# Attention, capacity MoE and a cosine MLP on one core: expert products of 448 columns, routing counts shared by two engines, an earlier gate

## The chip, the core and the metric

The kernel runs on one core of a Trainium2 chip. The metric is the device time of one execution in microseconds (us): the time before is the median of three runs, 1180.96 us (1175.52 to 1181.75). A profiled execution stands beside them.

## What is computed

Three stages follow one another, all in float32 (the reference, cut to what matters):

```python
# attention: q, k, v are (4, 12, 448, 64)
q_n, k_n = rmsnorm(q, g_q), rmsnorm(k, g_k)
attn = softmax(q_n @ k_n.T / 8)            # rows normalised
x = (attn @ v) as (1792, 768)              # 4*448 tokens, 12*64 features

# capacity MoE: 8 experts, each takes at most 224 of the 1792 tokens
logits = x @ w_gate
# all (token, expert) pairs in falling order of logit: a token goes to the
# first expert that still has room
for e in range(8):
    out[mask_e] = relu(x[mask_e] @ w1[e]) @ w2[e]   # 768 -> 1024 -> 768

# cosine MLP: 768 -> 2048 -> 768
h = out @ w_in
return (h * cos(h)) @ w_out
```

Every expert ends with exactly 224 tokens, since 8 times 224 is 1792.

## The kernel before, in words

**Order of the work.** Nothing is issued as it is written. Each piece of work is a `Step` of a `Plan` (line 51): `add` notes what a step reads and writes, `cost` (line 65) estimates its length, and `run` (line 172) makes one list schedule of all steps: for each engine it takes, of the steps that can start first, the one with the earliest due time (`late`). The order is fixed when the program is built; at run time every engine runs its own list strictly in that order. `rush` and `ahead` bring a step's due time forward; `ahead` is left out for steps of the vector engine (line 119). The steps of `chain` (the expert and MLP products) stay in program order.

**The attention stage** takes the first third of the time. The change does not touch it, except that one more constant is set at its start. Then come four groups of two experts, each followed by the MLP for the group's 448 tokens.

**Splitting into high and low parts.** A float32 product is made from reduced-precision parts: a value is split in a high part (its rounding to the type FP32R) and a low part (what is left). `weights` (line 1210) loads 128 columns of an expert's weight from DRAM into a `ws` buffer (ring of 4; loads are issued by SyncE's queue, line 1205), makes the high part on ScalarE (line 1214, now and then on VectorE) and the low part with a subtraction on VectorE, both into a `wx` buffer (ring of 4). `three` (line 1241) then multiplies: high weight by high rows, high weight by low rows, low weight by high rows, three matmuls of 224 columns into one PSUM bank. Each matmul loads its own 128x128 weight. I call these three matmuls a block.

**An expert** (`expert`, line 1246) has two halves. In the first, 8 groups (`f`) of 6 blocks give the hidden rows; ScalarE applies Relu to the sum into the high part `hT[:, f, 0:CAP]`, and VectorE subtracts for the low part. In the second, 6 groups (`d`) of 8 blocks give the expert's output, split in the same way into `x2h` and `x2l`. So an expert has 96 blocks. Expert 0's first half is different: it uses plain float32 products (48 single matmuls) and no split. High and low rows of the input lie beside each other, in `xe[:, d, 0:448]`, and so do those of the hidden rows, in `hT[:, f, 0:448]`.

**The MLP** (`mlp`, line 1276) uses `three` as well, with 448 columns in each matmul, 16 groups of 6 blocks and then 6 groups of 16.

**Routing** runs in 8 phases (`Router.phase`, line 1029), one for each expert to be run: phase t settles one expert's tokens (`idx[t]`) and its number (`eid[t]`). Phases 0 and 1 take `quick`; phases 2 to 7 take `slow` (line 988). `slow` writes the tokens' best logits to DRAM (`rows`, line 996), reads them back spread over all partitions (`V`, shown as `AB` in the trace, eight loads, line 999, which wait for `rows`), both on SyncE's queue, and finds the threshold in 8 steps: compare 1792 candidates per partition as two halves of 896 (VectorE, into `oh`), add up each half (ScalarE, with `accum_out`), make `ind`, multiply it by a small matrix on TensorE, update `KX`. Then `M`, `pv` and `idx` follow, the phase's rows are gathered from DRAM on GpSimd's queue (`xr`, line 1165), transposed on TensorE and split into `xe`.

**When a phase may start.** `moe` calls `fetch(t)` for the second expert of a group while the first is planned; for the first expert of the next group it is called inside the MLP (`ahead()` at `d == TURN`), with `behind = chain[-EARLIER]`: phase 2, 4 or 6 may not start before that block is done, counted back from the last block of the group's second expert. `EARLIER` is 90, so the gate stands 6 blocks into the second expert.

The lines that the change touches:

```python
            for j in range(2):                                  # slow, lines 1008 to 1011
                z = junk[:, j * h:(j + 1) * h]
                v.tensor_scalar(z, V[:, j * h:(j + 1) * h], src.bitcast(F32), None, op0=ALU.is_ge)
                nc.scalar.activation(z, z, AF.Copy, accum_out=cnt[:, j:j + 1])
            P.tensor.matmul(p, hi, xh, start=first, stop=False) # three, lines 1242 to 1244
            P.tensor.matmul(p, hi, xl, start=False, stop=False)
            P.tensor.matmul(p, lo, xh, start=False, stop=last)
            behind = chain[-EARLIER]                            # moe
```

In the trace nearly all instructions carry line 47, that of the helper that records them; they are told apart by their tiles.

Of the kernel before, what the change touches and what calls it, by code (L numbers as in the profile page):

```python
# [12 lines left out]
F32 = mybir.dt.float32  # L13
F32R = mybir.dt.float32r
BF16 = mybir.dt.bfloat16
I32 = mybir.dt.int32
AF = mybir.ActivationFunctionType
ALU = mybir.AluOpType
# [32 lines left out]
class Plan:  # L51
# [13 lines left out]
    def cost(self, eng, name, out, r, kw):  # L65
        n = max([out.free_size()] + [x.free_size() for x in r])
        if eng == "PE":
            if self.key(out)[1]:
                return 0.055
            rhs = r[1] if name == "matmul" else r[0]  # L70
            passes = 1 if rhs.dtype != F32 else 4 if name == "matmul" else 2
            if name == "matmul" and rhs.dtype == F32 and self.beside:
                if out.partition_size() == 32:
                    return 0.05
                passes *= {32: 0.32, 64: 0.48}.get(out.partition_size(), 1)
            if self.halves:
                return 0.112
            if self.close and name == "transpose":
                return 0.105
            return max(out.free_size() / 2333.0 + 0.011, 0.107 if rhs.dtype == F32R else 0.0467) * passes  # L80
        small = sum(1 for x in r if x.free_size() == 1) if n > 1 else 0
        if eng == "ACT":
            return (0.05 if any(x.space == bass.MemoryType.PSUM for x in r) else 0.093) + n / 1200.0 + 0.093 * (
                ("accum_out" in kw) + small)
        if eng == "POOL":
            if name in ("memset", "tensor_copy"):
                return 0.035 + n * 0.00083 if name == "memset" else 0.1 + n * 0.00345
            if name == "tensor_tensor" and any(s == 0 for x in r for s, _ in list(x.ap)[1:]):
                return 0.1 + n * 0.00176
            two = name == "tensor_scalar" and "op1" in kw  # L90
            return 0.1 + n * {"iota": 0.0015, "tensor_scalar": 0.0054 if two else 0.00375,
                              "scalar_tensor_tensor": 0.0014}.get(name, 0.00217)
        if name == "memset":
            return 0.008 + n / 960.0
        fast = name in ("tensor_scalar", "tensor_copy") and "accum_out" not in kw and not any(
            x.space == bass.MemoryType.PSUM for x in r)
        return 0.068 + n / (1920.0 if fast else 960.0) + small * (0.061 if name == "scalar_tensor_tensor" else 0.03)
# [53 lines left out]
    def ring(self, pool):  # L151

        def make(name, n, shape, dt=F32):
            tiles = [pool.tile(shape, dt, name=f"{name}{i}") for i in range(n)]
            at = [0]

            def take():
                at[0] += 1
                return tiles[(at[0] - 1) % n]
            return take  # L160
        return make
# [549 lines left out]
class Router:  # L711
# [3 lines left out]
    def __init__(self, nc, pool, ident, L, rows):  # L715
# [5 lines left out]
        def t(name, shape, dt=F32):  # L721
            P[name] = pool.tile(shape, dt, name=name)
            return P[name]
# [81 lines left out]
        g.memset(t("capE", [128, E]), BIG)  # L805
        v.tensor_copy(t("wd", [128, E]), w8)
        g.memset(t("rp", [128, 1]), float(CAP))
        g.memset(t("rp2", [128, 1]), 2.0 * CAP)
        self.first_free()
        for name in ("m", "mx", "K", "F0", "F1", "Z", "X0", "X1", "X2", "W0", "W1", "W2", "G", "Q", "X", "W", "g"):  # L810
# [177 lines left out]
    def slow(self):  # L988


        nc, P, v, ps = self.nc, self.P, self.nc.vector, self.psum
        vm, vt, V, junk, cnt = P["vm"], P["vt"], P["V"], P["junk"], P["cnt"]
        v.tensor_scalar(vt, P["oe"].rearrange("p c e -> p e c"), 2 * BIG, -BIG, op0=ALU.mult, op1=ALU.add)
        v.tensor_tensor(vm, vt, P["m"].unsqueeze(1).to_broadcast([CP, E, NCOL]), op=ALU.min)
        rows, sync = self.rows, nc.nc.sync
        nc.add([("SP", 0.5, lambda: sync.dma_start(rows.rearrange("e (p c) -> p e c", c=NCOL), vm))], [vm], ["rows"],
               dma=0.2, land=2.8)
        for e in range(E):
            nc.add([("SP", 0.85, lambda e=e: sync.dma_start(V[16 * e:16 * e + 16],
                                                           rows[e:e + 1].to_broadcast([16, NCOL * CP])))],  # L1000
                   ["rows"], [V[16 * e:16 * e + 16]], dma=0.4, land=8.0)
        b, KX, ti, h = P["b"], P["KX"], P["ti"], NCOL * CP // 2
        for s in range(8):
            src = P["b0"]
            if s:
                v.tensor_tensor(b, KX, P["ix"][:, s:s + 1], op=ALU.bitwise_xor)
                src = b
            for j in range(2):
                z = junk[:, j * h:(j + 1) * h]
                v.tensor_scalar(z, V[:, j * h:(j + 1) * h], src.bitcast(F32), None, op0=ALU.is_ge)  # L1010
                nc.scalar.activation(z, z, AF.Copy, accum_out=cnt[:, j:j + 1])
            v.tensor_scalar(P["ind"], cnt[:, 0:1], cnt[:, 1:2], P["rp"], op0=ALU.add, op1=ALU.is_ge)
            p = ps()
            nc.tensor.matmul(p[:, 0:1], P["bd"].rearrange("p e i -> p (e i)"), P["ind"], start=True, stop=True)
            if s == 0:
                v.tensor_copy(ti, p[:, 0:1])
                v.tensor_scalar(ti, ti, 28, None, op0=ALU.logical_shift_left)
                self.flip(KX, ti, b)
            else:
                v.tensor_scalar(ti, p[:, 0:1], float(1 << (28 - 4 * s)), None, op0=ALU.mult)  # L1020
                v.tensor_tensor(KX, KX, ti, op=ALU.bitwise_xor)
        p = ps()
        nc.tensor.transpose(p[0:CP, 0:128], KX[:, 0:1].bitcast(F32).to_broadcast([128, CP]), self.ident)
        th = P["th"]
        v.tensor_reduce(th, p[0:CP, 0:128], AX.X, ALU.max)
        for j, op in enumerate((ALU.is_gt, ALU.is_equal)):
            v.tensor_scalar(P["M"][0:CP, :, j], vm, th, None, op0=op)
# [77 lines left out]
PT = 2 * CAP  # L1105
# [6 lines left out]
GATE = 2  # L1112
AHEAD = 100.0
TURN = 5
EARLIER = 90
MAGS = 4
GROUPS = [[0, 1], [2, 3], [4, 5], [6, 7]]

# [1 line left out]
def moe(tc, P, R, ident, x_rows, w1, w2, w_in, w_out, out, narrow):  # L1120

    nc = tc.nc
    with ExitStack() as ctx:
# [10 lines left out]
        rbuf = ring("r", 3, [128, PT])  # L1134
        kbuf = ring("k", 2, [128, PT], I32)
        obuf = ring("o", 1, [128, PT])
        rows = ring("xr", 2, [CP, DM])
        xe = cst.tile([128, KD, PT], F32R, name="xe")
        xf = cst.tile([128, KD, CAP], F32, name="xf")
# [95 lines left out]
        def block(f):  # L1235
            P.begin()
            f()
            P.finish()
            chain.append(P.steps[-1])

        def three(p, hi, lo, xh, xl, first, last):
            P.tensor.matmul(p, hi, xh, start=first, stop=False)
            P.tensor.matmul(p, hi, xl, start=False, stop=False)
            P.tensor.matmul(p, lo, xh, start=False, stop=last)

        def expert(t, j):
            def of(w):
                return lambda: w[bass.ds(ev[t], 1)].rearrange("o k n -> (o k) n")

            for f in range(K1):  # L1250
                if t == 0:
                    s = whole(of(w1), f * 128, KD, [f"ev{t}"])
                    p = acc()[:, 0:CAP]
                    for d in range(KD):
                        block(lambda: P.tensor.matmul(p, s[:, d], xf[:, d], start=d == 0,
                                                      stop=d == KD - 1))
                else:
                    hi, lo = weights(of(w1), f * 128, KD, [f"ev{t}"])
                    p = acc()[:, 0:CAP]
                    for d in range(KD):  # L1260
                        block(lambda: three(p, hi[:, d], lo[:, d], xe[:, d, 0:CAP], xe[:, d, CAP:PT], d == 0,
                                            d == KD - 1))
                a, b = hT[:, f, 0:CAP], hT[:, f, CAP:PT]
                sc.activation(a, p, AF.Relu)
                v.scalar_tensor_tensor(b, p, 0.0, a.bitcast(F32), op0=ALU.max, op1=ALU.subtract)
            o = j * CAP
            for d in range(KD):
                hi, lo = weights(of(w2), d * 128, K1, [f"ev{t}"])
                p = acc()[:, 0:CAP]
                for f in range(K1):  # L1270
                    block(lambda: three(p, hi[:, f], lo[:, f], hT[:, f, 0:CAP], hT[:, f, CAP:PT], f == 0, f == K1 - 1))
                a, b = x2h[:, d, o:o + CAP], x2l[:, d, o:o + CAP]
                sc.activation(a, p, AF.Copy)
                v.tensor_tensor(b, p, a.bitcast(F32), op=ALU.subtract)
# [138 lines left out]
```

## Time and profile before

| What | Value |
|---|---|
| median of three runs | 1180.96 us (1175.52 to 1181.75) |
| the profiled execution's own time | 1176.82 us |
| its span, first to last instruction | 1174.9 us |
| mean granted clock of TensorE | 0.981 |
| TensorE matmul busy | 1126.4 us (96%) |
| TensorE weight load busy | 936.4 us (80%) |
| VectorE busy | 844.6 us (72%) |
| ScalarE busy | 653.0 us (56%) |
| GpSimd busy | 139.7 us (12%) |

All views below are of the profiled execution, whose own time is 1.9 us over its span. PE is TensorE's matmul, PEld its weight load, DVE is VectorE, ACT ScalarE, POOL GpSimd, SP SyncE; a q behind the name means the engine's queue, which waits or issues a DMA. Matmuls are pipelined, so a row's busy time shows when an engine has work and not how fast it goes: the rate is read from how many matmuls start in a stretch. A few matmul records can be missing.

### The profile page before, as it was taken

How to read it: one execution, taken by the hardware profiler on the slowest of the kernel's cores; microseconds unless marked ns; L12 is line 12 of the kernel's file. 1: busy time of each engine (PE TensorE's matmuls, PEld its weight loads, DVE VectorE, ACT ScalarE, POOL GpSimd, SP SyncE). 2: the span in 40 equal slices, each digit the busy share in tenths (PEclk: the TensorE clock that was granted, in tenths of full speed). 3: DMA queues.
4: the chain of work that ended last, by engine and by line, in shares of the span. 5: the costliest groups of instructions: out<-in, count | busy, mean ns of one | idle time of the engine just before them, and what ended most of it. 6: DMA issues, size and time to landing. Idle time of an engine off the chain costs nothing.

```text
span 1174.9 us, 23429 instructions
## 1 busy us (share of the span) xinstructions
PE 1126.4 (96%) x8664; PEld 936.4 (80%) x8664; DVE 844.6 (72%) x2327; ACT 653.0 (56%) x1565; POOL 139.7 (12%) x287
## 2 busy tenths in 40 slices
PE   7999999999994999999999999999999999999996
PEld 5555565555543899889899989899999989999996
DVE  6888998999978876995877588377688457646401
ACT  4778788676662345873645584355477254536400
POOL 5352331331000000000001000002000000100001
PEclk9999999999996899999999999999999999999998
DMA  8236575655661579879668868929966955856761
GB/s 212 63 103 222 150 230 189 194 170 175 231 205 63 148 220 250 301 244 282 206 155 243 224 212 245 314 88 244 244 213 232 310 183 154 249 194 217 251 215 48
DMA packets 180818, 237.66 MB, mean 202 GB/s; under 512 B 14112, under 2 KB 156896, under 8 KB 175072
## 3 DMA queue, kind: packets, MB, share of 16 engines
q1 hardware_dynamic: 178144, 225.15, 63.0%
q0 software_dynamic: 2560, 11.01, 3.1%
q8 instruction: 68, 1.11, 0.4%
q14 instruction: 46, 0.38, 0.1%
HBM read 199.52 MB, written 36.52 MB: 201 GB/s over the span
## 4 chain that ended last, share of the span: by engine, by line
PE 78%; DVE 11%; DMA 5%; ACT 3%; issue 1%; POOL 1%; SPq 1%; POOLq 0%; DVEq 0%; ACTq 0%
PE acc L47 55%; PE st L47 6%; PE po L47 5%; PE dn L47 3%; PE s L47 3%; PE t L47 3%; DMA ws<-in_moe_w_dram 2%; DVE cm L47 2%; DVE na L47 1%; PE rt L47 1%; PE tr L47 1%; PE dn L418 1%; DVE oh L47 1%; DMA rows<-vm 1%; DVE AB L47 1%
## 5 line engine op out<-in xcount | busy, mean ns | idle before, releaser
L47 PE MATMUL acc<-gh,wx 128*128 128x224 f32 (+1 forms) x1952 | 365.5, 312 | 0.3 <-DVE wx L47 0.2
L47 PEld LDWEIGHTS acc<-gh,wx 128*128 128x128 f32 x1952 | 279.6, 191 | 11.2 <-DVE wx L47 0.7
L47 PE MATMUL acc<-x2h,wx 128*128 128x448 f32 x768 | 223.1, 369 | 0.0
L47 DVE TENSOR_TENSOR wx<-ws,wx 128x768 fp32r<-128x768 f32 (+1 forms) x104 | 112.3, 1080 | 67.8 <-ACT wx L1214 63.0
L47 PEld LDWEIGHTS acc<-x2h,wx 128*128 128x128 f32 x768 | 144.5, 188 | 12.8 <-issue 1.2
L1214 ACT ACTIVATE wx<-ws 128x768 fp32r<-128x768 f32 (+1 forms) x102 | 96.4, 945 | 98.4 <-PE acc L47 55.9
L47 PE MATMUL acc<-gl,wx 128*128 128x448 f32 (+1 forms) x400 | 143.0, 357 | 0.0
L47 PE MATMUL acc<-x2l,wx 128*128 128x448 f32 x384 | 140.3, 365 | 0.0
L47 ACT ACTIVATE oh<-oh 128x896 bf16<-128x896 bf16 x96 | 90.5, 943 | 68.7 <-DVE oh L47 68.5
L47 PE MATMUL acc<-xe,wx 128*128 128x224 f32 x1008 | 114.4, 275 | 0.0
L47 PEld LDWEIGHTS acc<-xe,wx 128*128 128x128 f32 x1008 | 113.6, 192 | 0.1
L47 ACT ACTIVATE pf<-st 112x448 f32<-112x448 f32 x192 | 93.8, 539 | 35.2 <-PE st L47 34.4
L47 DVE TENSOR_REDUCE cm<-s 128x1 f32<-128x448 f32 x168 | 100.0, 617 | 15.8 <-PE s L47 13.8
L47 ACT ACTIVATE r<-r 128x448 f32<-128x448 f32 x128 | 73.2, 575 | 44.8 <-DVE r L47 43.3
L47 PE MATMUL st<-qq,kk 64*112 64x448 f32 x576 | 89.7, 389 | 0.9 <-ACT pf L47 0.9
L1165 POOL DMA_INDIRECT xr<-x,idx x16 | 15.8, 990 | 603.0 <-issue 199.0
L47 PE MATMUL po<-pf,vr 112*64 112x448 f32 x384 | 83.4, 552 | 0.3 <-ACT pf L47 0.3
L47 PEld LDWEIGHTS acc<-gl,wx 128*128 128x128 f32 x400 | 75.5, 189 | 4.6
L47 PEld LDWEIGHTS acc<-x2l,wx 128*128 128x128 f32 x384 | 72.2, 188 | 5.4
L47 DVE TENSOR_SCALAR oh<-AB,b 128x896 bf16<-128x896 f32 x96 | 61.8, 682 | 14.1 <-DMA AB<-rows 12.8
L47 PEld LDWEIGHTS st<-qq,kk 64*112 64x112 f32 x576 | 49.5, 172 | 18.4 <-ACT pf L47 5.4
L47 ACT ACTIVATE sq<-qk 112x64 f32<-112x64 f32 (+1 forms) x195 | 57.5, 302 | 9.3 <-DMA qk<-in_k_dram 6.6
(245 smaller groups left out, 1692.7 us busy)
## 6 DMA issues: line engine op xcount, KB each, us to landing
wx<-w_in SPq DMA_DIRECT2D x64, 768.0 KB
wx<-w_out SPq DMA_DIRECT2D x44, 1024.0 KB
ws<-in_moe_w_dram SPq DMA_DIRECT2D x64, 384.0 KB
ws<-in_moe_w_dram SPq DMA_DIRECT2D x48, 512.0 KB
nr<-in_moe_w_in_dram SPq DMA_DIRECT2D x32, 384.0 KB
w_in<-nr SPq DMA_DIRECT2D x32, 384.0 KB
nr<-in_moe_w_out_dram SPq DMA_DIRECT2D x16, 512.0 KB
w_out<-nr SPq DMA_DIRECT2D x16, 512.0 KB
```

What stands on the lines that cost most here:

```text
L47: self.plan.add([(self.eng, self.plan.cost(self.eng, name, out, r, kw), lambda: f(*args, **kw))], r, w)
L418: lambda: nc.tensor.matmul(pw[:, 0:256], wz[:, 0:128], wz, start=True, stop=True))], [wz], [pw])
L1165: P.add([("POOL", 2.1 - 0.9 * h, lambda x=x, h=h: nc.gpsimd.indirect_dma_start(out=x, out_offset=None, in_=x_rows, in_offset=bass.Indirect ...
L1214: P.add([("ACT", 0.093 + n * 0.1067, lambda: nc.scalar.activation(hi, s, AF.Copy)), ("DVE", 0.07 + n * 0.0667, lambda: nc.vector.tensor_co ...
```

## The change

`two` takes the place of `three` in the experts: one matmul of the high weight with all 448 columns (high rows and low rows side by side) and one of the low weight with the 224 high rows, added onto the first 224 columns. The sum then lies in two halves of a bank; `halves` copies the second to SBUF (ScalarE) and adds the first to it (VectorE) into a new ring `sm` of two buffers, and what followed reads that. Expert 0's first half and the MLP keep their form. In `slow` the second half of each comparison becomes one VectorE instruction that compares and sums; a constant `one` is set for it. `EARLIER` goes from 90 to 140: the gate stands 50 blocks sooner. The plan's estimate for a short FP32R matmul goes from 0.107 to 0.112 us.

```diff
--- before.py
+++ after.py
@@ -77,7 +77,7 @@
                 return 0.112
             if self.close and name == "transpose":
                 return 0.105
-            return max(out.free_size() / 2333.0 + 0.011, 0.107 if rhs.dtype == F32R else 0.0467) * passes
+            return max(out.free_size() / 2333.0 + 0.011, 0.112 if rhs.dtype == F32R else 0.0467) * passes
         small = sum(1 for x in r if x.free_size() == 1) if n > 1 else 0
         if eng == "ACT":
             return (0.05 if any(x.space == bass.MemoryType.PSUM for x in r) else 0.093) + n / 1200.0 + 0.093 * (
@@ -805,6 +805,7 @@
         g.memset(t("capE", [128, E]), BIG)
         v.tensor_copy(t("wd", [128, E]), w8)
         g.memset(t("rp", [128, 1]), float(CAP))
+        g.memset(t("one", [128, 1]), 1.0)
         g.memset(t("rp2", [128, 1]), 2.0 * CAP)
         self.first_free()
         for name in ("m", "mx", "K", "F0", "F1", "Z", "X0", "X1", "X2", "W0", "W1", "W2", "G", "Q", "X", "W", "g"):
@@ -1005,10 +1006,11 @@
             if s:
                 v.tensor_tensor(b, KX, P["ix"][:, s:s + 1], op=ALU.bitwise_xor)
                 src = b
-            for j in range(2):
-                z = junk[:, j * h:(j + 1) * h]
-                v.tensor_scalar(z, V[:, j * h:(j + 1) * h], src.bitcast(F32), None, op0=ALU.is_ge)
-                nc.scalar.activation(z, z, AF.Copy, accum_out=cnt[:, j:j + 1])
+            z, y = junk[:, 0:h], junk[:, h:2 * h]
+            v.tensor_scalar(z, V[:, 0:h], src.bitcast(F32), None, op0=ALU.is_ge)
+            nc.scalar.activation(z, z, AF.Copy, accum_out=cnt[:, 0:1])
+            v.scalar_tensor_tensor(y, V[:, h:2 * h], src.bitcast(F32), P["one"].to_broadcast([128, h]), op0=ALU.is_ge,
+                                   op1=ALU.mult, accum_out=cnt[:, 1:2])
             v.tensor_scalar(P["ind"], cnt[:, 0:1], cnt[:, 1:2], P["rp"], op0=ALU.add, op1=ALU.is_ge)
             p = ps()
             nc.tensor.matmul(p[:, 0:1], P["bd"].rearrange("p e i -> p (e i)"), P["ind"], start=True, stop=True)
@@ -1112,7 +1114,7 @@
 GATE = 2
 AHEAD = 100.0
 TURN = 5
-EARLIER = 90
+EARLIER = 140
 MAGS = 4
 GROUPS = [[0, 1], [2, 3], [4, 5], [6, 7]]
 
@@ -1134,6 +1136,7 @@
         rbuf = ring("r", 3, [128, PT])
         kbuf = ring("k", 2, [128, PT], I32)
         obuf = ring("o", 1, [128, PT])
+        sums = ring("sm", 2, [128, CAP])
         rows = ring("xr", 2, [CP, DM])
         xe = cst.tile([128, KD, PT], F32R, name="xe")
         xf = cst.tile([128, KD, CAP], F32, name="xf")
@@ -1243,6 +1246,16 @@
             P.tensor.matmul(p, hi, xl, start=False, stop=False)
             P.tensor.matmul(p, lo, xh, start=False, stop=last)
 
+        def two(p, hi, lo, x, first, last):
+            P.tensor.matmul(p, hi, x, start=first, stop=False)
+            P.tensor.matmul(p[:, 0:CAP], lo, x[:, 0:CAP], start=False, stop=last)
+
+        def halves(p):
+            y = sums()
+            sc.activation(y, p[:, CAP:PT], AF.Copy)
+            v.tensor_tensor(y, p[:, 0:CAP], y, op=ALU.add)
+            return y
+
         def expert(t, j):
             def of(w):
                 return lambda: w[bass.ds(ev[t], 1)].rearrange("o k n -> (o k) n")
@@ -1256,19 +1269,20 @@
                                                       stop=d == KD - 1))
                 else:
                     hi, lo = weights(of(w1), f * 128, KD, [f"ev{t}"])
-                    p = acc()[:, 0:CAP]
+                    p = acc()[:, 0:PT]
                     for d in range(KD):
-                        block(lambda: three(p, hi[:, d], lo[:, d], xe[:, d, 0:CAP], xe[:, d, CAP:PT], d == 0,
-                                            d == KD - 1))
+                        block(lambda: two(p, hi[:, d], lo[:, d], xe[:, d], d == 0, d == KD - 1))
+                    p = halves(p)
                 a, b = hT[:, f, 0:CAP], hT[:, f, CAP:PT]
                 sc.activation(a, p, AF.Relu)
                 v.scalar_tensor_tensor(b, p, 0.0, a.bitcast(F32), op0=ALU.max, op1=ALU.subtract)
             o = j * CAP
             for d in range(KD):
                 hi, lo = weights(of(w2), d * 128, K1, [f"ev{t}"])
-                p = acc()[:, 0:CAP]
+                p = acc()[:, 0:PT]
                 for f in range(K1):
-                    block(lambda: three(p, hi[:, f], lo[:, f], hT[:, f, 0:CAP], hT[:, f, CAP:PT], f == 0, f == K1 - 1))
+                    block(lambda: two(p, hi[:, f], lo[:, f], hT[:, f], f == 0, f == K1 - 1))
+                p = halves(p)
                 a, b = x2h[:, d, o:o + CAP], x2l[:, d, o:o + CAP]
                 sc.activation(a, p, AF.Copy)
                 v.tensor_tensor(b, p, a.bitcast(F32), op=ALU.subtract)
```

## Rows read from the trace of the kernel before

**Rows 1.** The page's first part: busy time, share of the span, instructions.

```profile
PE 1126.4 (96%) x8664; PEld 936.4 (80%) x8664; DVE 844.6 (72%) x2327; ACT 653.0 (56%) x1565; POOL 139.7 (12%) x287
```

**Rows 2.** Busy time by stretch (stretch, length, engines, granted clock, DMA share, GB/s).

```profile
core 0: us, PE busy (x) PEld busy (x) DVE busy (x) ACT busy (x) POOL busy (x), PEclk, DMA share, GB/s
465.00:481.00 16.00, 14.67 (x86) 13.20 (x86) 14.63 (x36) 12.30 (x25) 0.00 (x0) 1.00 1.05 391
...
595.20:612.30 17.10, 17.10 (x163) 17.10 (x162) 15.16 (x56) 8.83 (x15) 1.87 (x2) 1.00 0.66 175
...
645.90:662.30 16.40, 16.33 (x146) 16.12 (x144) 7.92 (x13) 6.84 (x13) 0.00 (x0) 1.00 1.02 243
...
711.00:764.00 53.00, 53.00 (x278) 48.28 (x278) 28.52 (x104) 19.47 (x38) 1.91 (x2) 1.00 0.92 282
...
1011.60:1027.70 16.10, 16.10 (x147) 16.10 (x146) 10.15 (x16) 8.83 (x16) 0.76 (x2) 1.00 0.86 255
```

**Rows 3.** Chain that ended last, in order of time (start us, us, what).

```profile
534.70 17.13 PE acc L47 x84
...
816.00 37.20 PE acc L47 x333
```

**Rows 4.** TensorE's groups by shape: the matmuls of 224 columns.

```profile
L47 PE MATMUL acc<-gh,wx 128*128 128x224 f32 x1216 | 146.6, 276 | 0.3 <-DVE wx L47 0.2
...
L47 PE MATMUL acc<-xe,wx 128*128 128x224 f32 x1008 | 114.4, 275 | 0.0
```

**Rows 5.** Timeline from 645 us, where expert 3's second half begins (start us, us).

```profile
645.88 4.29 PE L47 MATMUL acc<-gh,wx 128*128 128x224 f32 x37
646.09 0.36 ACT L47 ACTIVATE gh<-acc 128x224 fp32r<-128x224 f32 x1 [0.70 <-PE acc L47]
646.34 1.05 ACT L1214 ACTIVATE wx<-ws 128x1024 fp32r<-128x1024 f32 x1
646.56 0.38 DVE L47 SCALAR_TENSOR_TENSOR gh<-acc,gh 128x224 fp32r<-128x224 f32 x1
647.42 1.23 DVE L47 TENSOR_TENSOR wx<-ws,wx 128x1024 fp32r<-128x1024 f32 x1 [0.48 <-ACT wx L1214]
```

**Rows 6.** VectorE's and ScalarE's groups by shape (busy us, mean ns, idle before).

```profile
L47 DVE TENSOR_SCALAR oh<-AB,b 128x896 bf16<-128x896 f32 x96 | 61.8, 682 | 14.1 <-DMA AB<-rows 12.8
...
L47 DVE SCALAR_TENSOR_TENSOR r<-r,acc 128x448 f32<-128x448 f32 x64 | 39.0, 616 | 19.6 <-ACT r L47 19.5
...
L47 ACT ACTIVATE oh<-oh 128x896 bf16<-128x896 bf16 x96 | 90.5, 943 | 68.7 <-DVE oh L47 68.5
...
L47 ACT ACTIVATION_READ_ACCUMULATOR oh<-oh 128x1 f32 x96 | 17.9, 187 | 0.0
```

**Rows 7.** TensorE's waits after 360 us (total us, times, longest).

```profile
PE rt L47 <- DVE ind L47: 1.1, 2, 0.6
```

**Rows 8.** Timeline: phase 5's second gather on GpSimd, and its first use.

```profile
797.42 0.94 POOL L1165 DMA_INDIRECT xr<-x,idx  x1 [0.30 <-PE acc L47]
...
807.19 0.55 PE L47 MATMUL tr<-ident,xr 112*128 112x112 f32 x4
```

**Rows 9.** Timeline of phase 4's start on VectorE and of SyncE's queue.

```profile
631.33 0.28 DVE L47 TENSOR_TENSOR La<-L,capE 112x128 f32<-112x128 f32 x1
...
638.29 0.89 SPq L996 DMA_DIRECT2D rows<-vm  x1
...
641.04 1.23 DVE L47 TENSOR_TENSOR wx<-ws,wx 128x1024 fp32r<-128x1024 f32 x1 [0.96 <-ACT wx L1214]
...
643.99 3.57 SPq L999 DMA_DIRECT2D AB<-rows  x8
...
647.80 1.04 SPq L1205 DMA_DIRECT2D ws<-in_moe_w_dram  x2
```

**Rows 10.** Chain that ended last, 440 to 470 us and 636 to 660 us.

```profile
454.39 9.38 DMA ws<-in_moe_w_dram
...
647.80 6.81 DMA ws<-in_moe_w_dram
```

**Rows 11.** GpSimd's groups of the first 20 us.

```profile
L47 POOL MEMSET rp<- 128x1 f32 x2 | 0.1, 98 | 0.0
```

## The prediction

> **What bounds the kernel now.** I read the page first: TensorE is busy for 96% of the span, the other engines far less [rows 1]. As a busy matmul row tells nothing of the rate, I went on to the busy times by stretch, to see what TensorE does in the stage that changes. In the experts' halves the weight load (PEld) is busy without a pause, 17.10 of 17.10 us and 16.10 of 16.10, while in the MLP it is busy 48.28 of 53.00 [rows 2]: so an expert's matmuls wait for their weights, and the MLP's do not. The granted clock is 1.00, the 2.4 GHz level, in all these stretches. Next the chain that ended last, which gives the rate of either kind of matmul in a stretch without other work: 333 of 224 columns in 37.20 us, 111.7 ns each, and 84 of 448 columns in 17.13 us, 203.9 ns each [rows 3]. Twice the columns cost 1.83 times as much. Last, I looked for TensorE's idle time behind 445 us: 1.33 us between 465 and 481, 0.07 us in expert 3's second half, almost none elsewhere [rows 2]. The bound is TensorE, and what the change takes from it counts in full unless something becomes late that now is not.
>
> **Blocks.** The change replaces three matmuls of 224 by one of 448 and one of 224. Seven experts have 48 blocks in the first half (3 x 336 = the 1008 matmuls that read xe), eight have 48 in the second (1152 of the 1216 that read gh; the other 64 are in the MLP's last group) [rows 4]: 720 blocks. Before, one costs 3 x 111.7 = 335.1 ns; after, 203.9 + 111.7 = 315.6 ns. That is 19.5 ns less, 14.0 us in all. No row shows the two shapes in turn. Bounds: the pair costs what its 672 columns cost now, 335.1 ns, and nothing is gained; or both go at the 448 rate of 0.455 ns a column, 305.9 ns, and 21.1 us are gained. I take 14.0, since either shape has a row of its own.
>
> The Trainium skill, "TensorE: Matmul & The Clock Gate", gives a weight load of 128 columns 107 ns (LDWEIGHTS) and a warm matmul N/2.4 + 2.5 ns (Back-to-back issue gap). By that a 224 matmul is held by its load and a 448 one takes 189 ns: block 320 before, 296 after, an estimate of 17 us for 720. The measured 111.7 agrees with the first to 5 ns; the measured 203.9 stands 15 ns above the second, and I follow the rows.
>
> **Two more instructions per group.** 7 x 8 + 8 x 6 = 104 groups get a copy from PSUM on ScalarE (0.36, as the Relu) and an addition on VectorE (0.38, as the subtraction that also reads PSUM and SBUF) [rows 5]: 37 and 40 us more work, beside TensorE. What hides it: four PSUM banks and weights that are ready some groups ahead. In an expert's first half without routing VectorE is busy 10.15 of 16.10 us; 8 x 0.38 makes it 13.2 of 15.2. In expert 2's first half it is 15.16 of 17.10 [rows 2], as phase 3's end falls there; 3 us more would be 18.2 in about 16.2, so without an earlier end of that phase three such halves lose 2 us each.
>
> Where the latency shows is the step from the first half to the second: the last hidden rows are wanted by the eighth block. Now: half two starts at 645.88, the rows are wanted 7 x 335.1 ns = 2.35 us later, at 648.23; Relu at 646.09 and the subtraction that ends at 646.94 leave 1.29 us [rows 5]. After: 0.36 + 0.38 and two handovers of 0.11 (646.45 to 646.56) more, 0.96, in a window that is 0.14 shorter; 0.19 us are left. But ScalarE takes a weight copy of 1.05 right behind, and VectorE a low part of 1.23 [rows 5]; in a two-step eviction either can come between. So a wait of 0 to 2.1 us at each of seven such places (expert 0 has none), 0 to 14.7 in all. The schedule puts what is due first in front but can't interrupt: I take half of a ScalarE copy, 0.5 us each, 3.5 us.
>
> **Counting.** Per comparison one pass of ScalarE goes (943 + 187 ns), and one of VectorE turns from 682 ns to a scalar_tensor_tensor of 896; one of 448 takes 616 [rows 6], so at most twice that, 1.23, and at least 0.68. With 48 comparisons VectorE gets 0 to 26 us, ScalarE loses 54. The second half no longer stands behind the first on ScalarE, so a step may end up to 1.13 us sooner and a phase 9 us. I cost this at nothing: TensorE waits for `ind` 1.1 us in the whole stage [rows 7], and the tightest phases, the odd ones, send the second gather at 797.42, 9.8 us ahead of its first transpose [rows 8]. If that cover went, experts would start late; an earlier end widens it. The extra constant is one GpSimd memset of 98 ns [rows 11], ahead of the warm-up at the worst: 0 to 0.1 us. The plan's 0.112 for a short matmul issues nothing and lies nearer to the measured 111.7: nothing, within the noise of a new order.
>
> **The gate.** 50 blocks sooner is 50 x 0.3156 = 15.8 us. What moves: `La` and the phase's VectorE work, but also nine DMAs on SyncE's queue, `rows` and eight `AB` loads that wait for it, with the weight loads behind them. Today phase 4 starts at 631.33, issues `rows` at 638.29 and the `AB` loads at 643.99 to 647.56 [rows 9]. A weight load whose buffer came free at 642.27 (641.04 + 1.23) was issued at 647.80 [rows 9] and took 6.81 us [rows 10]: 12.3 us from free to landed, and TensorE stood for only 0.07 us. It is one of the expert's last two loads. 15.8 us sooner the block meets loads of the first half, whose groups last 6 x 0.3156 = 1.9 us, not 2.7: four buffers cover 12.3 x 1.9/2.7 = 8.7 us there. Bounds over the three even phases: today's 1.4 us of idle go (-1.4), or each has the whole 9.3 us of queue (638.29 to 647.56) and the longest landing of such a load, 9.38 [rows 10]: 18.7 - 8.7 = 10 us each, 30 - 1.4 = +28.6. I take a delay of 1.3 us each, about a tenth of the way, since 12.3 us cost no more than 0.07 today: 3.9 - 1.4 = +2.5. VectorE's comparisons then fall partly beside experts; they have no `ahead` and stand behind weights. GpSimd's gathers come after the last group's scatters either way.
>
> **Sum.** 1176.8 - 14.0 + 3.5 + 2.5 = 1168.8 us against the profiled execution's own time, which is 4.1 below the median of the runs shown; those spread over 6.2. I put half of the difference on top: 1171 us.
>
> **Rivals.** *The eviction gives the gain back.* At each of the seven steps both waits fall in: 14.7 in place of 3.5, 1180 + 2 = 1182. For it speaks the 0.19 us that are left, against it that due work goes first.
>
> *Slower: SyncE's queue starves the experts.* With the earlier gate three even phases block the weight loads of the second expert's first half: 28.6 in place of 2.5 gives 1195 + 2 = 1197. It decides from a free-to-landed time over 8.7 us, and today's is 12.3. Against it: today's landing of 6.81 in place of 9.38 would take a quarter off, and not every phase need meet the worst place.
>
> *A larger gain.* The pair runs at the 448 rate, no step waits, today's 1.4 go: 1176.8 - 21.1 - 1.4 = 1154 + 2 = 1156. By the skill's figures above, the blocks would give 17 of it.
>
> *It doesn't do what it says.* A pair costs what three did, because load and matmul alternate otherwise than in like rows: 1176.8 + 3.5 + 2.5 = 1183 + 2 = 1185.
>
> **Chances.** Forecast 0.60 (its own range 1160 to 1176), eviction 0.14, queue 0.12, larger gain 0.08, no shorter pair 0.06. The range 1160 to 1185 leaves out the queue and the larger gain, 0.20. About 0.5%, 5.9 us, is what a measurement of this kernel can tell: faster is below 1175.1, which the forecast gives but for its edge (0.02) and the larger gain too: 0.66. Same: eviction, no shorter pair and a little of the rest, 0.21. Slower: the queue and 0.01 of the edge, 0.13.
>
> **What would show it.** In the profile after: 720 matmuls of 448 and 720 of 224 where 2160 of 224 were, and stretches of the chain at 158 ns a matmul in the experts; half as many `oh` passes on ScalarE; expert halves near 15.2 us where they are 16.1. A wait of TensorE for `gh` at each second half shows the eviction rival; weight loads issued late behind `AB` in a first half, with TensorE waiting for `wx`, the queue. I am wrong if pairs take 335 ns, or if TensorE's idle time behind 445 us exceeds 14 us.

## The result and the profile after

The changed kernel takes 1167.94 us (median of 5 runs, 1162.75 to 1169.76) where the kernel before, in runs beside it, took 1177.97: a ratio of 0.9902, 95% interval 0.9883 to 0.992. That is 1% faster. The forecast was 1171, faster. The sum lay near; two of its terms did not, as the experiments show.

The page of the profiled execution (1162.75 us, span 1160.8 us), engines' busy time as in [rows 1]:

```profile
PE 1108.4 (95%) x7944; PEld 906.6 (78%) x7944; DVE 899.8 (78%) x2477; ACT 646.4 (56%) x1575; POOL 137.6 (12%) x288
```

TensorE has 720 matmuls fewer (8664 to 7944), as counted, VectorE has 55 us more work, ScalarE 7 us less. The profiled execution was the fastest of the five. It is 14.1 us below the profiled one of before, and some 3 us of that lie in the attention stage, which runs the same instructions but for the one constant: phase 0's first count of the settled tokens is on TensorE at 371.5 us in place of 374.8. Over the profiles of all the runs below it stands anywhere from 370.2 to 376.7. So I read the gain from the runs, and from single profiles only what happens inside a stage.

First the pair. A stretch of the changed kernel's timeline in expert 7's first half, where no routing is left (start us, us, engine, instruction, count):

```profile
999.47 15.20 PE L47 MATMUL acc<-xe,wx 128*128 128x448 f32 x96
1014.51 1.73 PE L47 MATMUL acc<-gh,wx 128*128 128x448 f32 x10
```

From the first start to the next stretch's start are 15.04 us for 48 pairs: 313 ns each, where three matmuls took 335 and I had reckoned with 315.6. For 720 pairs that is 15.7 us less.

Then TensorE's idle time. The stretches of experts 3, 5 and 7 from late in the expert before to the MLP (columns as in [rows 2]):

```profile
core 0: us, PE busy (x) PEld busy (x) DVE busy (x) ACT busy (x) POOL busy (x), PEclk, DMA share, GB/s
621.00:654.00 33.00, 31.15 (x196) 28.79 (x195) 25.72 (x54) 20.28 (x44) 1.89 (x4) 1.00 0.84 244
811.00:843.00 32.00, 30.37 (x191) 28.13 (x190) 25.08 (x53) 19.85 (x42) 1.19 (x4) 1.00 0.84 250
1000.00:1031.00 31.00, 31.00 (x197) 29.43 (x196) 21.59 (x40) 18.62 (x40) 0.64 (x2) 1.00 0.81 234
```

TensorE stands still for 1.85 us with expert 3 and 1.63 us with expert 5, and not at all with expert 7, behind which no phase is left. Where it waits with expert 3, the timeline of ScalarE and VectorE shows the last two groups of hidden rows on their way:

```profile
638.24 0.39 DVE L47 TENSOR_TENSOR sm<-acc,sm 128x224 f32<-128x224 f32 x1
638.41 0.36 ACT L47 ACTIVATE sm<-acc 128x224 f32<-128x224 f32 x1
...
639.19 1.07 ACT L1217 ACTIVATE wx<-ws 128x1024 fp32r<-128x1024 f32 x1 [0.42 <-DMA ws<-in_moe_w_dram]
639.67 0.38 DVE L47 TENSOR_TENSOR sm<-acc,sm 128x224 f32<-128x224 f32 x1
640.16 0.65 ACT L47 ACTIVATE gh<-sm 128x224 fp32r<-128x224 f32 x2
...
641.43 0.69 DVE L47 SCALAR_TENSOR_TENSOR gh<-sm,gh 128x224 fp32r<-128x224 f32 x2
```

The additions of both groups are done at 638.63 and 640.05. The Relu of the first could start then, but ScalarE's list has a weight copy in front of it, and that copy waits for its load. Both Relus run at 640.16, both subtractions at 641.43, behind another weight's low part, and TensorE, which wants these rows, waits. The chain that ended last, from the phase's `AB` loads on SyncE's queue (618.71, from the queue's timeline) to TensorE's next matmul, shows where the late load comes from:

```profile
618.71 4.07 SPq L1000 DMA_DIRECT2D AB<-rows  x8
```

```profile
623.66 8.30 DMA ws<-in_moe_w_dram
...
631.99 0.85 ACT wx L1217
...
632.87 0.84 DVE wx L47
...
633.86 5.31 DMA ws<-in_moe_w_dram
...
639.19 1.07 ACT wx L1217
...
641.43 0.40 DVE gh L47
...
641.87 3.29 PE acc L47 x19
```

The weight load issued at 623.66, the second one behind the `AB` loads (out at 622.78), took 8.30 us; its buffer, split by 633.83, was the one that the next load was waiting for. That one landed at 639.17, and its copy is the one in front of the Relu. VectorE had made the last split before the issue by 622.21, so the queue held the load for 1.5 us at most, and the landing was the longer part of its lateness. The `AB` loads, which stood at 643.99 [rows 9], now meet the loads of expert 3's first half, as the prediction had it.

The comparisons, and the copies and additions of the pairs, by shape (busy us, mean ns, idle before):

```profile
L47 DVE SCALAR_TENSOR_TENSOR oh<-AB,b,one 128x896 bf16<-128x896 f32 x48 | 55.0, 1146 | 0.0
L47 DVE TENSOR_TENSOR sm<-acc,sm 128x224 f32<-128x224 f32 x104 | 39.8, 386 | 13.1 <-ACT sm L47 12.8
...
L47 ACT ACTIVATE oh<-oh 128x896 bf16<-128x896 bf16 x48 | 45.6, 950 | 73.8 <-DVE oh L47 73.7
L47 ACT ACTIVATE sm<-acc 128x224 f32<-128x224 f32 x104 | 36.4, 353 | 38.5 <-PE acc L47 35.3 <-PE rt L47 2.4
```

The instruction that compares and sums takes 1146 ns, inside the bounds of 0.68 to 1.23 us. Last, the cover of an odd phase: its second gather and first transpose, as in [rows 8], of the changed kernel:

```profile
780.77 0.93 POOL L1168 DMA_INDIRECT xr<-x,idx  x1 [0.30 <-issue]
...
798.18 0.55 PE L47 MATMUL tr<-ident,xr 112*128 112x112 f32 x4
```

From the end of the gather's issue to the transpose are 16.5 us, where they were 8.8 (798.36 to 807.19). The experiments show that this number decides whether the pairs pay.

### The profile page after: what moved, and what is told of

The parts are those of the page before. It is cut to its first block, busy times and chain, and to the rows that moved or that the text cites. A ratio compares the mean times of both kernels' runs of the same rounds, so it can differ in the third digit from the quotient of the medians.

```text
span 1160.8 us, 22190 instructions
## 1 busy us (share of the span) xinstructions
PE 1108.4 (95%) x7944; PEld 906.6 (78%) x7944; DVE 899.8 (78%) x2477; ACT 646.4 (56%) x1575; POOL 137.6 (12%) x288
## 4 chain that ended last, share of the span: by engine, by line
PE 45%; DVE 3%; DMA 2%; ACT 1%; issue 1%; POOL 0%; POOLq 0%; SPq 0%; ACTq 0%; DVEq 0%
PE acc L47 44%; DMA ws<-in_moe_w_dram 2%; PE tr L47 1%; DVE wx L47 1%; DVE na L47 1%; ACT wx L1217 1%; PE rt L47 1%; DVE oh L47 0%; DVE xo L47 0%; POOL out_dram L1337 0%; DVE xe L47 0%; POOLq L1423 0%; DVE gh L47 0%; DVE ind L47 0%; DVE sm L47 0%
## 5 line engine op out<-in xcount | busy, mean ns | idle before, releaser
L47 PE MATMUL acc<-gh,wx 128*128 128x448 f32 (+1 forms) x1568 | 360.4, 344 | 4.1 <-DVE gh L47 3.6
L47 PEld LDWEIGHTS acc<-gh,wx 128*128 128x128 f32 x1568 | 264.8, 190 | 22.1 <-DVE gh L47 5.8
L47 DVE TENSOR_REDUCE cm<-s 128x1 f32<-128x448 f32 x168 | 100.2, 618 | 14.1 <-PE s L47 12.1
L47 PE MATMUL acc<-xe,wx 128*128 128x448 f32 (+1 forms) x672 | 107.3, 320 | 0.1
L47 PEld LDWEIGHTS acc<-xe,wx 128*128 128x128 f32 x672 | 100.6, 189 | 5.3 <-DVE wx L47 0.6
L47 ACT ACTIVATE oh<-oh 128x896 bf16<-128x896 bf16 x48 | 45.6, 950 | 73.8 <-DVE oh L47 73.7
L1168 POOL DMA_INDIRECT xr<-x,idx x16 | 15.5, 966 | 582.7 <-issue 198.8
L47 DVE COPY xo<-tr 112x512 f32<-112x512 f32 (+1 forms) x25 | 16.5, 664 | 58.0 <-PE tr L47 56.4
```

The source lines that it names most:

```text
L47: self.plan.add([(self.eng, self.plan.cost(self.eng, name, out, r, kw), lambda: f(*args, **kw))], r, w)
L1168: P.add([("POOL", 2.1 - 0.9 * h, lambda x=x, h=h: nc.gpsimd.indirect_dma_start(out=x, out_offset=None, in_=x_rows, in_offset=bass.Indirect ...
```

## Experiments

Each edit is against the kernel before or the changed one, as said; each was timed in five rounds against the kernel before. Ratios are to that kernel, with 95% intervals.

**One part alone.** The pairs alone (the two helpers, their calls and the ring, nothing else):

```diff
+            P.tensor.matmul(p, hi, x, start=first, stop=False)
+            P.tensor.matmul(p[:, 0:CAP], lo, x[:, 0:CAP], start=False, stop=last)
...
-                    p = acc()[:, 0:CAP]
+                    p = acc()[:, 0:PT]
...
+                    p = halves(p)
```

> The experts' pairs with their halves added, and nothing else of the change (comparisons, gate at 90 and plan estimate as before). Theory (the pairs carry the gain): 720 blocks of about 314 ns in place of 335, 14 to 15 us, less waits where an expert's second half begins, 0 to 5 us: 1163 to 1169 where the kernel before takes 1178. Rival (the earlier gate and the shared counting bring the gain, the pairs lose theirs to the longer eviction): within 3 us of 1178.

Measured: 1183.79 us, ratio 1.004 (1.0021 to 1.0058). The theory fell: the pairs by themselves make the kernel 5 us slower (4 by the medians). TensorE's waits in this kernel (engine, tile, line, what for, total us, times, longest):

```profile
PE tr L47 <- DMA xr<-x,idx: 10.9, 6, 2.7
PE acc L47 <- DVE gh L47: 1.9, 3, 0.7
```

For hidden rows, behind the longer eviction, TensorE waits 1.9 us. The 10.9 us are new: it waits for the gathered rows of the odd phases, twice in each. Phase 5's tokens and gather in the timeline, and the busy time of the three stretches in which phases 3, 5 and 7 end:

```profile
802.03 0.17 DVE L47 CAST idx<-row 112x2 int32<-112x2 f32 x1
802.96 3.27 POOL L1166 DMA_INDIRECT xr<-x,idx  x1 [71.05 <-DVE eid L47]
806.53 1.90 POOL L1166 DMA_INDIRECT xr<-x,idx  x1 [0.30 <-issue]
...
811.09 0.60 PE L47 MATMUL tr<-ident,xr 112*128 112x112 f32 x4 [1.05 <-DMA xr<-x,idx]
811.46 0.86 PE L47 MATMUL acc<-gh,wx 128*128 128x448 f32 x4
815.06 0.60 PE L47 MATMUL tr<-ident,xr 112*128 112x112 f32 x4 [2.74 <-DMA xr<-x,idx]
815.43 2.04 PE L47 MATMUL acc<-gh,wx 128*128 128x448 f32 x8
```

```profile
605.00:628.00 23.00, 19.34 (x120) 17.96 (x119) 16.95 (x41) 10.84 (x22) 10.43 (x10) 0.85 0.80 234
800.00:823.00 23.00, 19.08 (x123) 17.76 (x124) 17.95 (x43) 11.44 (x24) 10.03 (x10) 0.93 0.77 234
997.00:1017.00 20.00, 16.50 (x94) 15.24 (x93) 14.13 (x32) 9.92 (x21) 10.00 (x10) 0.83 0.82 249
```

The gather's issue ends at 808.43, 10 us later than before (798.36), although expert 4 began at 782.2 and not at 786.2. The phases slip on the way: phase 4's `rows` is issued at 644.3 (638.29 before), phase 5 has its tokens at 802.03, 6.8 us later than before:

```profile
795.26 0.16 DVE L47 CAST idx<-row 112x2 int32<-112x2 f32 x1
```

The other 3.3 us are the gather's own: its two issues take 3.27 and 1.90 us, where the kernel before has 0.94 each; why is open. It is tempting to blame VectorE's 40 us of additions for the slip; the run with a longer landing, below, speaks against it. Of 8.8 us of cover 2.7 are left, and the rows have not landed when TensorE, which keeps its list's order, comes to the transposes. TensorE stands for 3.7, 3.9 and 3.5 us in the three stretches, and the granted clock falls to 0.85, 0.93 and 0.83: behind the wait of 2.74 us the eight matmuls from 815.43 take 1.84 us to the next transpose, where four pairs at the 2.4 GHz level take 1.25.

The shared counting alone (the diff's edit of `slow`, and the constant):

```diff
-            for j in range(2):
...
+            v.scalar_tensor_tensor(y, V[:, h:2 * h], src.bitcast(F32), P["one"].to_broadcast([128, h]), op0=ALU.is_ge,
+                                   op1=ALU.mult, accum_out=cnt[:, 1:2])
```

> Half of the comparisons summed by VectorE, and nothing else of the change. Theory (routing is covered): phases end some 6 us sooner, TensorE's time stays, 1178 within 3 us. Rival (routing's length is on the path): 3 to 8 us faster. Rival (VectorE is short of time): 3 us or more slower.

Measured: 1179.94, ratio 1.0003 (0.9982 to 1.0024). As expected: worth nothing alone, though phase 5 sends its second gather 12.5 us sooner than before (797.42):

```profile
784.93 0.93 POOL L1167 DMA_INDIRECT xr<-x,idx  x1 [0.30 <-issue]
```

More cover buys nothing where there was enough.

The gate alone:

```diff
-EARLIER = 90
+EARLIER = 140
```

> EARLIER at 140 in place of 90, and nothing else of the change. Theory (the block in SyncE's queue meets weight loads of the second expert's first half): TensorE waits there for weights, 0 to 4 us slower than 1178. Rival (an earlier phase relieves the MLP stage): 2 us or more faster.

Measured: 1182.56, ratio 1.0035 (1.0014 to 1.0055), 4 us slower. The size fits; but the profiled execution was its fastest (1174.63 us) and shows no wait for weights, so where the runs lose it is open.

So three edits give +5, 0 and +4 us alone, and with the plan's estimate -12 together. The next runs take one back at a time, from the changed kernel.

**All but one.** The gate back at 90:

```diff
-EARLIER = 140
+EARLIER = 90
```

> The changed kernel with the gate back at 90: pairs, shared counting, plan estimate. In the pairs alone TensorE waits 10.9 us for the gathered rows of the odd phases. Theory A (what ends an odd phase late is its eight comparison steps, so the shared counting alone gives the cover back): 1166 to 1171, waits for the gather under 3 us. Theory B (an odd phase starts late because the even one before it does, so the gate gives the cover back): 1178 to 1184, waits for the gather over 6 us.

Both halves of a comparison summed by ScalarE again (the counting's edit undone), with the rest of the change:

> The changed kernel with both halves of a comparison summed by ScalarE again: pairs, gate at 140, plan estimate. Theory A (the counting gives the cover back): 1178 to 1184, waits for the gather over 6 us. Theory B (the gate does): 1166 to 1171, waits for the gather under 3 us.

Three matmuls again, with the rest of the change (the pairs' edit undone):

> The changed kernel with three matmuls of 224 in the experts again: shared counting, gate at 140 and plan estimate alone. Theory (these three only give the pairs their cover and are worth nothing by themselves): 1177 to 1184, so that the pairs, put on top, are worth 10 to 15 us. Rival (they bring a part of the gain themselves): 1170 to 1175.

Measured: gate at 90, 1175.24, ratio 0.9971 (0.9953 to 0.9988); no shared counting, 1178.69, ratio 0.9996 (0.9979 to 1.0013); no pairs, 1180.95, ratio 1.0017 (0.9998 to 1.0036). The waits for the gather of the first and of the second:

```profile
PE tr L47 <- DMA xr<-x,idx: 3.5, 3, 2.4
```

```profile
PE tr L47 <- DMA xr<-x,idx: 4.9, 3, 3.8
```

Neither theory holds by itself: the second run's time lies in theory A's range, but neither wait lies in the range of a theory. Phase 5's second gather in the first and in the second:

```profile
796.71 0.94 POOL L1168 DMA_INDIRECT xr<-x,idx  x1 [0.30 <-issue]
```

```profile
803.80 1.45 POOL L1166 DMA_INDIRECT xr<-x,idx  x1 [0.30 <-issue]
```

With both it goes at 780.77. The counting or the gate alone brings the wait from 10.9 down to 3.5 or 4.9 us, and each kernel has other losses; together they clear the odd phases, where no such wait is left behind 425 us. With the gate at 90 TensorE also waits 6.0 us for MLP weights: phase 5's `AB` loads hold SyncE's queue from 724.76 us, and a `w_out` load behind them takes 9.87 us (queue and chain of that kernel):

```profile
724.76 7.84 SPq L1000 DMA_DIRECT2D AB<-rows  x8
```

```profile
733.14 9.87 DMA wx<-w_out
```

The third run settles what the pairs are worth: with counting, gate and the plan's estimate in place they take the kernel from 1.0017 to 0.9902, 1.15% or 13.6 us, of the 15.7 that 720 pairs of 313 ns come to.

**The plan's order.** The plan's estimate back at 0.107:

```diff
-            return max(out.free_size() / 2333.0 + 0.011, 0.112 if rhs.dtype == F32R else 0.0467) * passes
+            return max(out.free_size() / 2333.0 + 0.011, 0.107 if rhs.dtype == F32R else 0.0467) * passes
```

> The changed kernel with the plan's old estimate of 0.107 us. Theory (the estimate only shifts the order a little): 1168 within 3 us. Rival (the estimate sets where transposes and counts are put between the products): over 4 us slower.

Measured: 1171.68, ratio 0.9944 (0.9925 to 0.9964). This is the rival's direction, 4 us by the medians and 5 by the ratios, so at its bound or just over: the intervals of this and of the changed kernel do not meet. It is also the three edits without the fourth: -7 us. TensorE waits 4.4 us for hidden rows here and 2.1 us for `ind`; which of the moved steps does it is not settled.

Then the pairs alone once more, but with the plan told that a gather lands later:

```diff
-                    land=5.0)
+                    land=5.0 if t < 2 else 12.0)
```

> The pairs alone (three of the four edits undone), but the plan believes that a gather of phases 2 to 7 lands 12 us after its issue in place of 5, so it puts the transposes of the gathered rows later in TensorE's list. Theory (the pairs alone lose their gain because TensorE, in its fixed order, reaches the transposes before the rows have landed, and drops to the 1.2 GHz level while it waits): waits for the gather fall from 10.9 us to under 3, the rest stays, 1166 to 1174. Rival (VectorE, which has more to do, holds the experts up wherever the transposes stand): 1180 or more.

Measured: 1174.99, ratio 0.996 (0.9942 to 0.9977). Of TensorE's waits behind 425 us those for the gather are gone, others are left:

```profile
PE acc L47 <- DVE gh L47: 6.3, 5, 2.2
PE acc L47 <- DVE rp L47: 2.4, 2, 1.3
```

One number, which moves no work but in the lists, makes 8.8 us of difference to the pairs alone, from 1183.8 to 1175.0. This shows that what ate the pairs' gain was TensorE's fixed order meeting a gather that had not landed. It is 1 us over the range that I gave; what remains in the list are waits for hidden rows and for a small step of VectorE's.

But the cure did not work as I had meant it. Phase 5 in this run:

```profile
790.87 0.17 DVE L47 CAST idx<-row 112x2 int32<-112x2 f32 x1
...
793.31 0.94 POOL L1166 DMA_INDIRECT xr<-x,idx  x1 [0.30 <-issue]
...
809.58 0.35 PE L47 MATMUL tr<-ident,xr 112*128 112x112 f32 x2
```

The first transpose stands no later in TensorE's list: 30 pairs into expert 4's second half, where with the pairs alone it stood 32 pairs in. The gather went earlier instead: its issue ends at 794.25 and not at 808.43. The plan counts due times back from the use, with the landing in between, so a longer landing makes the phase's steps due sooner. VectorE has the same work in both kernels (876.7 and 878.3 us busy), the 40 us of additions among it, and yet phase 5 has its tokens 4.4 us before the kernel of before. So it is not the length of the additions that makes the phase late, but the order of the lists.

The same edit for phase 1, on the changed kernel, where TensorE waits 2.6 us near 419 us:

```diff
-                    land=5.0)
+                    land=9.0 if t == 1 else 5.0)
```

> The changed kernel, but the plan believes that phase 1's gather lands 9 us after its issue in place of 5, so that TensorE's list reaches its transposes later. Theory (in the changed kernel TensorE waits 2.6 us for this gather near 419 us, and runs some products at the 1.2 GHz level behind it, because the plan takes the landing for too short): the wait falls under 0.5 us, 2 to 4 us faster than the changed kernel's 1168. Rival (expert 1's first half then waits for its rows, or the new order costs as much elsewhere): within 2 us of 1168.

Measured: 1168.24, ratio 0.99 (0.9877 to 0.9923): the same as the changed kernel. That wait is gone from the list, but waits for `ind` (1.6 us) and for other tiles took its place. The rival holds.

**The waits at second halves.** The last group of the first half with three matmuls and the short eviction, on the changed kernel:

```diff
+                    if f == K1 - 1:
+                        p = acc()[:, 0:CAP]
...
+                            block(lambda: three(p, hi[:, d], lo[:, d], xe[:, d, 0:CAP], xe[:, d, CAP:PT], d == 0,
...
+                    else:
```

> The changed kernel, but the last of the 8 groups of an expert's first half keeps its three matmuls and the short eviction. Theory (TensorE waits at the second half's start for the last hidden rows, 1.5 us each with experts 3 and 5, because of the longer eviction): these waits shrink to under 0.3 us, 7 x 6 blocks lose 21 ns each (0.9 us), net 1 to 3 us faster than the changed kernel's 1168. Rival (the wait is for weights that are late behind routing, not for the eviction): the waits stay, and the kernel is 1 us slower than the changed one.

Measured: 1170.24, ratio 0.9926 (0.9903 to 0.9949). The waits for hidden rows stay (columns as above):

```profile
PE acc L47 <- DVE gh L47: 4.1, 6, 1.3
```

So the length of the last eviction alone is not what TensorE waits for. This fits the chain above, where a Relu stands behind a weight copy that waits for its load.

The routing's nine DMAs from GpSimd's queue:

```diff
-        rows, sync = self.rows, nc.nc.sync
+        rows, sync = self.rows, nc.nc.gpsimd
...
-        nc.add([("SP", 0.5, lambda: sync.dma_start(rows.rearrange("e (p c) -> p e c", c=NCOL), vm))], [vm], ["rows"],
+        nc.add([("POOL", 1.0, lambda: sync.dma_start(rows.rearrange("e (p c) -> p e c", c=NCOL), vm))], [vm], ["rows"],
...
-            nc.add([("SP", 0.85, lambda e=e: sync.dma_start(V[16 * e:16 * e + 16],
+            nc.add([("POOL", 1.0, lambda e=e: sync.dma_start(V[16 * e:16 * e + 16],
```

> The changed kernel with the nine routing DMAs of a slow phase (rows and the eight AB loads) issued from GpSimd's queue in place of SyncE's. Theory (weight loads held behind them in SyncE's queue, and ScalarE's work queued behind a late weight, make TensorE's waits of 1.5 us at the second halves of experts 3 and 5): these waits go, 2 to 6 us faster than the changed kernel's 1168. Rival (the two-step eviction alone makes them): the waits stay, 1168 within 2 us.

Measured: 1198.83, ratio 1.0173 (1.0143 to 1.0202), 20 us slower than the kernel before; a miss for both. And the eight `AB` loads as one DMA on SyncE's queue:

```diff
-        for e in range(E):
-            nc.add([("SP", 0.85, lambda e=e: sync.dma_start(V[16 * e:16 * e + 16],
...
+        nc.add([("SP", 0.85, lambda: sync.dma_start(V, rows.unsqueeze(1).to_broadcast([E, 16, NCOL * CP])))],
+               ["rows"], [V], dma=3.2, land=8.0)
```

> The changed kernel with the eight AB loads of a slow phase as one DMA with a repeating source, so that SyncE's queue is held for one issue in place of eight (3.6 us before). Theory (weight loads behind that block are late in the second experts' first halves, and cause the waits for hidden rows of some 2 us each with experts 3 and 5): these waits shrink by half or more, 1 to 4 us faster than the changed kernel's 1168. Rival (the two-step eviction makes them whatever the weights do): 1168 within 1.5 us.

Measured: 1189.48, ratio 1.0083 (1.0058 to 1.0108), slower as well. Pieces of the chain, of the kernel with GpSimd's queue and of the one with one load:

```profile
636.72 11.64 DMA ws<-in_moe_w_dram
...
734.63 18.28 DMA wx<-w_out
```

```profile
633.60 9.27 DMA AB<-rows
642.88 9.93 DMA ws<-in_moe_w_dram
```

SyncE's queue is free in the first and held for one issue in the second, and yet expert weights of 512 KB near the `AB` loads take 11.64 and 9.93 us, where such a load took 6.81 in the kernel before [rows 10]. The `w_out` load is twice as large and was issued behind four others; with the gate at 90 one took 9.87. So a weight load is late not only because it is issued late; near the `AB` transfers it is also slow. How the two share what was lost is not separated by these runs. In the kernel with one load TensorE waits longest for the routing itself:

```profile
PE rt L47 <- DVE ind L47: 9.2, 3, 3.5
```

None of these versions beats the changed kernel.

## Why the prediction was right, and where it failed

*The bound.* Right. TensorE was the bound, and with the pairs' cover in place most of what they save there comes out: 13.6 of 15.7 us.

*Blocks.* Right, the gain sized a little low (14.0 us for 15.7): 315.6 ns a pair forecast, 313 measured, between the bounds of 305.9 and 335.1. The rival that a pair costs what three did is out.

*Two more instructions per group.* The sum, 3.5 us, was met (1.85 + 1.63 us of idle), but by luck. It was not half a microsecond at each of seven places, but two places, with experts 3 and 5, beside which an even phase runs, and none with expert 7. The mechanism named, a weight copy between the two steps, is what the timeline shows, with the addition that the copy itself waits for its load, which comes late behind the phase's DMAs: these 3.5 us belong to the gate as much as to the eviction. The 2 us that each of three first halves was to lose without an earlier end of the phase did not show: with the pairs alone expert 4's first half takes 15.5 us (782.21 to 797.69), 0.4 over 48 pairs. What the late phase cost came behind it, at the transposes.

*Counting.* Here the prediction failed. The step was "I cost this at nothing", with the cover of 9.8 us in front of an odd phase's first transpose. By itself the edit is worth nothing (1.0003). But I read the cover from the kernel before and did not ask what the pairs do to it: in the new lists the gather's issue ended 10 us later, while the first transpose, by its place in the list, stood only 3 us later. With the pairs in place the shared counting is worth 0.9996 against 0.9902, some 11 us. The text did say that if the cover went, experts would start late and that an earlier end widens it; it priced neither.

*The gate.* Its price of +2.5 us is near what it costs alone (1.0035, +4 us), and wrong in the company of the rest: from 0.9971 to 0.9902 it brings 8 us. The step that failed looked only at SyncE's queue, and took an earlier phase for something that nobody waits for. An earlier even phase lets the odd one behind it begin sooner, and that one has the deadline (phase 5's second gather at 780.77 in place of 796.71). The starving of the experts is there in kind, in the chain of expert 3, but at 3.5 us and not 30; these are the same 3.5 us as above.

*The plan's estimate.* Costed at nothing; it is worth 0.4%, by moving steps in the lists.

So the forecast of 1171 against 1167.94 is right in its main term, 14.0 us for 15.7. By the runs the change is 13.6 us for the pairs, less the 2 us, hardly clear of the noise, that the other three edits cost without them (1.0017); by the forecast it was 14.0 less 3.5 and 2.5. The sum came out in part by luck: the two edits that I took for free or for a cost are what let the main term come out. A kernel with the pairs alone would have been forecast at about 1168 by the same working, and takes 1184.

## What to carry to other kernels

When a bound shrinks, read every cover again with the new lengths: a phase that ended 9 us in time ended late once the lists were made anew around shorter products. In a fixed order an engine pays for a late operand where the list puts the first use, so one estimate that brings its producer forward can be worth as much as the edit itself: here 8.8 us, with no work moved but in the lists. Edits should be judged together and one by one: here three that gave +5, 0 and +4 us alone gave -7 together, and -12 with another estimate in the plan.

## What the runs showed of the hardware that I had not expected

In a mixed stream the 313 ns of a pair are below the sum of the two shapes' own rates, 203.9 + 111.7 = 315.6 ns: the two matmuls in turn lose nothing to each other.

A wait can cost more than itself: with the pairs alone, two waits for a gather of 1 to 2.7 us each, close together, brought the granted clock of the stretch to 0.83 to 0.93, and matmuls went on at the 1.2 GHz level for a while. It need not: with experts 3 and 5 of the changed kernel TensorE stood for 1.85 and 1.63 us in all, and the granted clock of these stretches stayed at 1.00.

Fewer or elsewhere issued DMAs were no relief: one repeating load in place of eight landed after 9.27 us and the 512 KB weight load behind it took 9.93; with the eight issued from GpSimd's queue such a load took 11.64 us.
